# Attention's softmax weights divided before the product with v, whose result comes out as columns of x; even and odd heads in one step

## The chip, the core and the metric

The kernel runs on one core of one Trainium2 chip. Five engines work beside each other, each through its own instructions in order: PE (TensorE, the matrix array, with its weight loads shown apart as PEld), DVE (VectorE), ACT (ScalarE), POOL (GpSimd) and SP, which here only issues DMAs. The metric is the device time of one execution in microseconds (us); smaller is better. The kernel before takes 1169.96 us, the median of 3 runs (1168.95 to 1172.43).

## The reference

Three parts follow each other: attention, and two feed-forward parts, the second with a gate over 8 experts. Only attention is touched by the change. Its core, cut to what matters (B = 2, H = 8, S = 576, D = 64):

```python
def sm_attn(qq, kk, vv):                       # softmax over all keys
    s = scale * np.matmul(qq, kk.transpose(0, 1, 3, 2))
    a = np.exp(s - np.max(s, axis=-1, keepdims=True))
    a = a / (np.sum(a, axis=-1, keepdims=True) + 1e-09)
    return np.matmul(a, vv)
q_d = q.reshape(B, H, S // 4, 4, D).mean(axis=3)   # the same for k_d, v_d
out_up = np.repeat(sm_attn(q_d, k_d, v_d), 4, axis=2)       # "global": 144 averaged positions
mask = np.abs(pos[:, None] - pos[None, :]) < 4              # "local": 7 neighbours of each position
attn = ...                                                   # softmax of the masked scores, as above
return out_up + np.matmul(attn, v)
```

Its output, with heads and head dimension joined to 512 columns, is x (1152 rows). The first feed-forward part computes `h = x @ w_in`, `g = h * tanh(softplus(h))`, `g @ w_out`; its weights come as 64-bit floats. The second part takes most of the time and follows the first.

## The kernel before, in words

x is kept transposed, 512 columns as 4 groups of 128 partitions, split into a high and a low part (`xhi`, `xlo`). Its 1152 rows are 12 **tiles** of 96 rows; three tiles are a group of 288 columns, on which the first feed-forward part runs: `gemm1` (L531, 12 matmuls a step) and `gemm2` (L555, 12 matmuls a step), three steps later. Steps s = 0 to 17 work on the first three groups; group g can only start when attention has made its three tiles.

So attention is cut in four: three tiles are made in the **start**, before step 0. The other nine are made in three **waves** beside steps 0 to 5, 6 to 11 and 12 to 17. A list of steps (`attn_steps`, `hb_steps`, `piped`) is handed out between the matmuls of `gemm1` and `gemm2` by `pump`; a scheduler at build time then sets each engine's order. Between the attention steps of the start, 8 small matmuls of `identb` (L471) each keep PE at work. In the start the 64-bit weights are also rebuilt as 32-bit ones, by one ACT instruction (L185) and three on DVE (L186, L188, L190) for each half block, and split into two parts by ACT (L197) and POOL (L198); three buffers hold what DMA brings for it.

A **local unit** (`lunit`) is one tile and four heads of one parity, so two units make a tile. Even heads lie on partitions 0 to 63 of `qT` and `kT`, odd heads on 64 to 127. A unit has three steps: `sc` adds a mask and scores into one PSUM bank (L380, L383), takes row maxima on DVE (L307) and exponentials on ACT (L311, one per head); `tr` turns the weights on PE (L391) and copies them out on ACT (`pt`, L393); `av` multiplies with v (L398), and DVE takes the reciprocal of the sum and multiplies with it (L318, L319). The sum comes out of that product as a 65th column, since v has a column of ones (a row of 1e-9 is added for the reference's small term). The second unit of a tile has a fourth step, `fin`: four transposes (L409) bring x into columns, DVE adds the global part (L415), ACT and DVE make `xhi` and `xlo` (L416, L417).

A **global unit** (`gunit`) does the same for two heads of one parity and one half of a batch (L330, L342, L345, L354); four units make a half, and `gout` turns its result into columns (L364, `odT`).

Each fp32 matmul stands in the trace as two records, each transpose as one.

Of the kernel before, what the change touches and what calls it, by code (L numbers as in the profile page):

```python
# [24 lines left out]
PB = 3  # L25
# [11 lines left out]
def attn_moe_moe_kernel(  # L37
# [64 lines left out]

    vwt = [at.tile([W + 1, H, D + 1], F32, name=f"vw{i}", bufs=1) for i in range(VWB)]
    pl = [at.tile([TQ, H // 2, W + 1], F32, name=f"pl{i}", bufs=1) for i in range(PB)]
    pg = [at.tile([SH, 2, 2, SH + 1], F32, name=f"pg{i}", bufs=1) for i in range(PB)]
    for x in pl:
        POOL.memset(x[:, :, W:W + 1], 1.0)
    for x in pg:
        POOL.memset(x[:, :, :, SH:SH + 1], 1.0)
    for x in vwt:  # L110
        POOL.memset(x[96:W + 1, :, 0:D], 0.0)
        POOL.memset(x[96:W + 1, :, D:D + 1], 1e-9)
        POOL.memset(x[0:W, :, D:D + 1], 1.0)
# [112 lines left out]
    raw4, turned, kT, kd, qT, qd, vd, vw, od, odT, xt = ({} for _ in range(11))  # L226
# [30 lines left out]
    def load_vw(t):  # L257
        b, t6, lo, hi = window(t)
        vw[t] = vwt[t % VWB]
        for a, n in ((0, TQ), (TQ, W - TQ)):  # L260
            dma_kv(out=vw[t][a:a + n, :, 0:D], in_=v[b, :, lo + a:lo + a + n, :].rearrange("h p d -> p h d"))
# [26 lines left out]
    def prep_v(b, half):  # L288


        src = raw4["v", b, half]
        x = new(at, [SH + 1, H, D + 1], F32, "vd")
        POOL.memset(x[64:SH + 1, :, 0:D], 0.0)
        POOL.memset(x[64:SH + 1, :, D:D + 1], 2e-9)
        POOL.memset(x[0:SH, :, D:D + 1], 4.0)
        for i in range(2):
            a, z = x[:SH, 4 * i:4 * i + 4, 0:D], src[:, 4 * i:4 * i + 4]
# [3 lines left out]
        vd[b, half] = x  # L301

    def softmax_in(s3, p, n, scale, tag):

        nh = s3.shape[1]
        nm = new(at, [n, nh], F32, tag)
        DVE.tensor_reduce(out=nm, in_=s3, axis=AX.X, op=ALU.max, negate=True)  # L307
        if scale != 1.0:
            DVE.tensor_scalar(out=nm, in0=nm, scalar1=scale, scalar2=None, op0=ALU.mult)
        for i in range(nh):  # L310
            x = ACT.activation(out=p[i], in_=s3[:, i, :] if scale == 1.0 else s3[:, i, :].rearrange("p (c k) -> p c k", c=2),  # L311
                               func=AF.Exp, bias=nm[:, i:i + 1], scale=scale)
            exps.append(x)
# [7 lines left out]
    def gunit(b, half, heads):  # L321

        u = {}
        nh = len(heads)
        o = 64 * (heads[0] % 2)

        def sc():
            bk = at_bank()
            for i, h in enumerate(heads):
                PE.matmul(out=bk[:SH, SD * i:SD * i + SD], lhsT=qd[b, half][o:o + D, h // 2, :],  # L330
                          rhs=kd[b][o:o + D, h // 2, :], start=True, stop=True)
            s3 = bk[:SH, 0:nh * SD].rearrange("p (a b) -> p a b", b=SD)
            u["p"] = pg[state["pg"] % PB]
            state["pg"] += 1
            softmax_in(s3, [u["p"][:, i, :, 0:SH] for i in range(nh)], SH, 1.0 / 128.0, "gm")

        def tr():
            bk = at_bank()
            for i in range(nh):
                for c in range(2):  # L340
                    j = 2 * i + c
                    PE.transpose(out=bk[:SH + 1, SH * j:SH * j + SH], in_=u["p"][:, i, c, :],  # L342
                                 identity=ident[:SH, :SH])
            u["pt"] = new(at, [SH + 1, 2 * nh * SH], F32, "pt", 3)
            ACT.activation(out=u["pt"], in_=bk[:SH + 1, 0:2 * nh * SH], func=AF.Copy)  # L345

        def av():
            if (b, half) not in od:
                od[b, half] = new(at, [SH, H, D], F32, "od", 1)
            bk = at_bank()  # L350
            for i, h in enumerate(heads):
                for c in range(2):
                    j = 2 * i + c
                    PE.matmul(out=bk[:SH, (D + 1) * i:(D + 1) * (i + 1)], lhsT=u["pt"][:, SH * j:SH * j + SH],  # L354
                              rhs=vd[b, c][:, h, :], start=(c == 0), stop=(c == 1))
            o3 = bk[:SH, 0:nh * (D + 1)].rearrange("p (a b) -> p a b", b=D + 1)
            normalise(o3, SH, nh, od[b, half][:, heads[0]:heads[-1] + 1:2, :], "gd")
        return [sc, tr, av]

    def gout(b, half):  # L360
        bk = at_bank()
        src = od[b, half].rearrange("p h d -> p (h d)")
        for j in range(KD):
            PE.transpose(out=bk[:, SH * j:SH * j + SH], in_=src[:, 128 * j:128 * j + 128], identity=ident[:SH, :SH])  # L364
        t = new(at, [128, KD, SH], F32, "odT", 1)
        odT[b, half] = t
        ACT.activation(out=t.rearrange("p a b -> p (a b)"), in_=bk[:, 0:KD * SH], func=AF.Copy)

    def lunit(t, par):
# [4 lines left out]
        o = 64 * par  # L374
        u = {}

        def sc():
            bk = at_bank()
            s3 = bk[:TQ, 0:4 * W].rearrange("p (a b) -> p a b", b=W)
            PE.matmul(out=s3, lhsT=identb[:TQ, :TQ],  # L380
                      rhs=maskb[:TQ, m0:m0 + W].unsqueeze(1).to_broadcast([TQ, 4, W]), start=True, stop=False)
            for i in range(4):
                PE.matmul(out=s3[:, i, :], lhsT=qT[b, half][o:o + D, i, TQ * t3:TQ * t3 + TQ],  # L383
                          rhs=kT[b][o:o + D, i, lo:hi], start=False, stop=(i == 3))
            u["p"] = pl[(2 * t + par) % PB]
            softmax_in(s3, [u["p"][:, i, 0:W] for i in range(4)], TQ, 1.0, "lm")

        def tr():
            bk = at_bank()
            for i in range(4):  # L390
                PE.transpose(out=bk[:W + 1, TQ * i:TQ * i + TQ], in_=u["p"][:, i, :], identity=ident[:TQ, :TQ])  # L391
            u["pt"] = new(at, [W + 1, 4 * TQ], F32, "pt", 3)
            ACT.activation(out=u["pt"], in_=bk[:W + 1, 0:4 * TQ], func=AF.Copy)  # L393

        def av():
            bk = at_bank()
            for i in range(4):
                PE.matmul(out=bk[:TQ, (D + 1) * i:(D + 1) * (i + 1)], lhsT=u["pt"][:, TQ * i:TQ * i + TQ],  # L398
                          rhs=vw[t][:, 2 * i + par, :], start=True, stop=True)
            if t not in xt:  # L400
                xt[t] = new(at, [TQ, H, D], F32, "x", 3)
            normalise(bk[:TQ, 0:4 * (D + 1)].rearrange("p (a b) -> p a b", b=D + 1), TQ, 4,
                      xt[t][:, par:par + 7:2, :], "ld")

        def fin():
            bk = at_bank()
            src = xt[t].rearrange("p h d -> p (h d)")
            for j in range(KD):
                PE.transpose(out=bk[:, TQ * j:TQ * j + TQ], in_=src[:, 128 * j:128 * j + 128],  # L409
                             identity=ident[:TQ, :TQ])  # L410
# [7 lines left out]
        return [sc, tr, av] + ([fin] if par else [])  # L418

    def piped(units):  # L420

        n = max(len(u) for u in units)
        dl = 1 if state["start"] else 2
        return [units[i - dl * s][s] for i in range(len(units) + dl * n) for s in range(n)
                if 0 <= i - dl * s < len(units) and s < len(units[i - dl * s])]

    def hb_steps(hb):
# [14 lines left out]
        st += piped([gunit(b, half, hs) for hs in ([0, 2], [1, 3], [4, 6], [5, 7])])  # L442
        return st + [partial(gout, b, half)]

    def attn_steps(t0, t1):
        st, units = [], []
        for t in range(t0, t1):
            if t % 3 == 0:
                st += piped(units) if units else []
                st += hb_steps(t // 3)  # L450
                units = []
            if t >= VWB:
                st.append(partial(load_vw, t))
            units += [lunit(t, 0), lunit(t, 1)]
# [18 lines left out]
    def start_steps():  # L473
# [3 lines left out]
        near = {(t, par): lunit(t, par) for t in range(3) for par in range(2)}  # L477
        first = [near[t, par][:3] for t in range(2) for par in range(2)]
        far = [gunit(0, 0, hs) for hs in ([0, 2], [1, 3], [4, 6], [5, 7])]
        st = brought("k", 0, 0) + brought("q", 0, 0) + [first[0].pop(0), first[1].pop(0)] + brought("k", 0, 1)  # L480
        st += [partial(prep_v, 0, 0), partial(prep_v, 0, 1)]
        st += piped(first[:2] + [far[0], first[2], far[1], first[3], far[2], near[2, 0][:3], far[3], near[2, 1][:3]])
        return st + [partial(gout, 0, 0)] + [near[t, 1][3] for t in range(3)]
# [421 lines left out]
```

## Time and profile before

| | |
|---|---|
| median of 3 runs | 1169.96 us (1168.95 to 1172.43) |
| profiled execution | 1170.61 us, its span 1168.8 us |
| PE busy | 1116.5 us, 96% of the span |
| DVE, ACT, POOL busy | 639.9, 520.9, 420.9 us |
| start (0 to 74.1 us), waves (74.1 to 217.6 us) | first `gemm1` of steps 0 and 18 |
| mean granted TensorE clock | 0.977 of full speed |

The profile is one execution, taken by the hardware profiler. The time of this execution is its span plus what lies around it (1.8 us). Busy time of PE and PEld overlaps, and the durations of matmuls are longer than the distance from one to the next, since they are pipelined: what a row of matmuls costs is read from the starts of its neighbours.

### The profile page before, as it was taken

To read this page: it belongs to the slowest core of one execution; us is meant where nothing else is said; L and a number is where in the kernel's file an instruction comes from. 1 tells how busy PE (TensorE), PEld (TensorE's weight loads), DVE (VectorE), ACT (ScalarE), POOL (GpSimd) and SP (SyncE) were. 2 spreads that over 40 slices of the span, in tenths; PEclk is the share of its full clock that TensorE was granted. 3 is DMA by queue.
4 is the path that set the end of the run, shared out by engine and by line. 5 is a ranking of instruction groups with operands and counts; after the bars stand their busy time and mean duration, and the time that the engine had idled before them with its cause. 6 is when DMAs were issued, how large, how long until landed. Compare 5 with 4: busy or idle time off the path is not lost.

```text
span 1168.8 us, 19396 instructions
## 1 busy us (share of the span) xinstructions
PE 1116.5 (96%) x7418; PEld 1019.9 (87%) x7418; DVE 639.9 (55%) x1399; ACT 520.9 (45%) x1333; POOL 420.9 (36%) x479
## 2 busy tenths in 40 slices
PE   7979899879999799999999999999999999999998
PEld 6868788879999788898899988998899889988997
DVE  4884554696658976436444444364444544544342
ACT  3556556566566563342424424434244243342430
POOL 3622422462462642552514405225044052240500
PEclk9789999999999799999999999999999999999999
DMA  8474300041010210201102112011121120111102
GB/s 195 148 198 81 69 23 1 3 145 53 2 54 1 73 55 1 72 19 54 51 23 72 38 36 73 19 55 37 37 73 37 36 73 19 54 37 37 37 1 81
DMA packets 60201, 63.54 MB, mean 54 GB/s; under 512 B 24204, under 2 KB 44620, under 8 KB 60108
## 3 DMA queue, kind: packets, MB, share of 16 engines
q1 hardware_dynamic: 60108, 62.30, 18.4%
q8 instruction: 58, 0.95, 0.3%
q14 instruction: 35, 0.29, 0.1%
HBM read 59.93 MB, written 2.36 MB: 53 GB/s over the span
## 4 chain that ended last, share of the span: by engine, by line
PE 85%; DVE 7%; DMA 4%; issue 1%; ACT 1%; POOL 1%; SPq 0%; ACTq 0%; DVEq 0%; POOLq 0%
PE w L834 34%; PE acc L795 25%; PE w L531 8%; PE acc L555 7%; PE w L795 4%; PE w L383 1%; DMA vw<-in_v_dram 1%; DMA raw<-in_moe_w_out_dram 1%; DMA raw<-in_moe_w_in_dram 1%; PE w L398 1%; PE w L330 1%; DVE raw L190 1%; PE w L391 1%; DVE sums L689 1%; DVE raw L188 1%
## 5 line engine op out<-in xcount | busy, mean ns | idle before, releaser
L834 PE MATMUL w<-wc,hhi 128*128 128x512 f32 x1152 | 362.2, 392 | 0.0
L834 PEld LDWEIGHTS w<-wc,hhi 128*128 128x128 f32 x1152 | 213.6, 188 | 41.9
L834 PE MATMUL w<-wc,hlo 128*128 128x512 f32 x576 | 225.7, 392 | 0.0
L707 POOL TENSOR_TENSOR wc<-raw,wc 128x512 fp32r<-128x512 f32 x64 | 82.7, 1314 | 371.7 <-ACT wc L706 370.9
L795 PE MATMUL acc<-thi,wb 128*128 128x288 f32 x768 | 169.2, 295 | 1.1 <-ACT u L782 0.6
L795 PE MATMUL acc<-xhi,wb 128*128 128x288 f32 x768 | 166.6, 297 | 1.9 <-DVE hlo L787 1.3
L845 DVE SCALAR_TENSOR_TENSOR yacc<-w,P,yacc 128x512 f32<-128x512 f32 x126 | 94.3, 749 | 132.6 <-PE w L834 132.6
L795 PEld LDWEIGHTS acc<-xhi,wb 128*128 128x128 f32 x768 | 128.4, 189 | 3.9 <-DVE hlo L787 1.8
L795 PEld LDWEIGHTS acc<-thi,wb 128*128 128x128 f32 x768 | 128.5, 188 | 3.3 <-ACT u L782 0.8
L834 PEld LDWEIGHTS w<-wc,hlo 128*128 128x128 f32 x576 | 108.1, 188 | 24.1
L782 ACT ACTIVATE p<-acc 128x288 f32<-128x288 f32 x128 | 52.6, 412 | 164.8 <-PE acc L795 161.5
L786 ACT ACTIVATE hhi<-acc 128x288 fp32r<-128x288 f32 x128 | 52.8, 413 | 139.7 <-PE acc L795 117.6
L795 PE MATMUL acc<-xlo,wb 128*128 128x288 f32 x384 | 114.0, 297 | 0.0
L795 PE MATMUL acc<-tlo,wb 128*128 128x288 f32 x384 | 113.1, 295 | 0.0
L695 POOL TENSOR_TENSOR wb<-sums,wb 128x256 fp32r<-128x256 f32 x128 | 98.0, 786 | 15.6 <-ACT wb L694 8.6
L512 POOL TENSOR_SCALAR me<-me 128x288 f32<-128x288 f32 x64 | 62.5, 976 | 112.4 <-ACT me L511 100.7
L695 POOL TENSOR_TENSOR wb<-raw,wb 128x256 fp32r<-128x256 f32 x96 | 71.9, 752 | 75.3 <-PE acc L795 41.5
L787 DVE SCALAR_TENSOR_TENSOR hlo<-acc,hhi 128x288 fp32r<-128x288 f32 x128 | 58.0, 454 | 62.4 <-ACT hhi L786 62.0
L531 PE MATMUL w<-xhi,hi 128*128 128x288 f32 x256 | 78.9, 309 | 7.9 <-ACT xhi L416 4.7
L555 PE MATMUL acc<-glo,hi 128*128 128x288 f32 x256 | 76.5, 310 | 7.3 <-DVE glo L519 4.5
L531 PE MATMUL w<-xlo,hi 128*128 128x288 f32 x256 | 77.9, 305 | 0.1
L531 PE MATMUL w<-xhi,lo 128*128 128x288 f32 x256 | 77.5, 303 | 0.0
(196 smaller groups left out, 2174.6 us busy)
## 6 DMA issues: line engine op xcount, KB each, us to landing
raw<-in_moe_w_dram SPq DMA_DIRECT2D x64, 512.0 KB
raw<-in_moe_w_in_dram SPq DMA_DIRECT2D x16, 512.0 KB
raw<-in_moe_w_out_dram SPq DMA_DIRECT2D x16, 512.0 KB
vw<-in_v_dram SPq DMA_DIRECT2D x12, 192.0 KB
raw<-in_v_dram SPq DMA_DIRECT2D x8, 288.0 KB
raw<-in_q_dram SPq DMA_DIRECT2D x12, 144.0 KB
out_dram<-yacc SPq DMA_DIRECT2D x6, 256.0 KB
raw<-in_k_dram SPq DMA_DIRECT2D x2, 576.0 KB
```

Of the source, the lines that this page charges most:

```text
L188: DVE.scalar_tensor_tensor(out=x, in0=hi, scalar=0x80000000, in1=x, op0=ALU.bitwise_and, op1=ALU.bitwise_or)
L512: POOL.tensor_scalar(out=e, in0=e, scalar1=EXP20, scalar2=None, op0=ALU.min)
L531: PE.matmul(out=bk, lhsT=a[:, kk, o], rhs=b[:, kk, c0:c0 + n], start=(i == 0), stop=(i == 3 * KD - 1))
L555: PE.matmul(out=bk, lhsT=a[:, h, o], rhs=b, start=(first and i == 0), stop=(end and i == 2))
L695: POOL.tensor_tensor(out=t[:, 1], in0=src[u][w], in1=f32(t[:, 0]), op=ALU.subtract)
L707: POOL.tensor_tensor(out=t[:, 1], in0=r[:, a], in1=f32(t[:, 0]), op=ALU.subtract)
L782: ACT.activation(out=t, in_=bk[u, b], func=AF.Copy)
L786: ACT.activation(out=hi, in_=y, func=AF.Relu)
L787: DVE.scalar_tensor_tensor(out=lo, in0=y, scalar=0.0, in1=f32(hi), op0=ALU.max, op1=ALU.subtract)
L795: PE.matmul(out=bk[u, b], lhsT=wb[2 * h + u, w][:, wz, kk, :], rhs=ops[xz][:, k + kk, o + c:o + c + NP], start=(m in (0, 1, 5) and i == 0) ...
L834: PE.matmul(out=bk, lhsT=a[:, f, 128 * j:128 * j + 128], rhs=w[:, b, :], start=(i == 0), stop=(i == 3 * FH - 1))
L845: DVE.scalar_tensor_tensor(out=y, in0=bk, scalar=p, in1=y, op0=ALU.mult, op1=ALU.add)
```

## The change

The weights are divided by their sums before they are turned: ACT's exponentials give their sums as a second output (`accum_out`), DVE adds 1e-9 (and multiplies by 4 for the global part), takes the reciprocal and multiplies the weights in SBUF. So the columns of ones and the memsets for them go. The product with v then has v as the operand that is loaded (`lhsT`) and the turned weights as the one that streams; its result lies as columns, head dimension on partitions. Even heads are written to partitions 0 to 63 and odd heads to 64 to 127 of one PSUM bank, which is x's layout: `fin` and `gout` have nothing to turn and are part of `av` now. One unit has both parities; their matmuls alternate between the halves of the array, in the scores by rows and in the product with v by columns. So there are half as many units with twice as much in each, and a weights buffer more. `piped` puts a unit's steps two apart, latest step first, and the start has an order written out by hand. Fewer steps there bring fewer of the matmuls of `identb`.

The diff, cut to its core:

```diff
-PB = 3
+PB = 4
-    vwt = [at.tile([W + 1, H, D + 1], F32, name=f"vw{i}", bufs=1) for i in range(VWB)]
...
+    vwt = [at.tile([W, H, D], F32, name=f"vw{i}", bufs=1) for i in range(VWB)]
...
+    def softmax(s3, p, scale, rows, tag):
+        n, nh, nk = s3.shape
+        nm, den = new(at, [n, nh], F32, tag + "m", 4), new(at, [n, nh], F32, tag + "d", 4)
         DVE.tensor_reduce(out=nm, in_=s3, axis=AX.X, op=ALU.max, negate=True)
         if scale != 1.0:
             DVE.tensor_scalar(out=nm, in0=nm, scalar1=scale, scalar2=None, op0=ALU.mult)
         for i in range(nh):
+            exps.append(ACT.activation(out=p[:, i], in_=s3[:, i], func=AF.Exp, bias=nm[:, i:i + 1], scale=scale,
+                                       accum_out=den[:, i:i + 1]))
+        DVE.tensor_scalar(out=den, in0=den, scalar1=1e-9, scalar2=rows, op0=ALU.add, op1=ALU.mult)
+        DVE.reciprocal(out=den, in_=den)
+        DVE.tensor_tensor(out=p, in0=p, in1=den.unsqueeze(2).to_broadcast([n, nh, nk]), op=ALU.mult)
-    def normalise(o3, n, nh, dst, tag):
-        rec = new(at, [n, nh, 1], F32, tag)
-        DVE.reciprocal(out=rec, in_=o3[:, :, D:D + 1])
-        DVE.tensor_tensor(out=dst, in0=o3[:, :, 0:D], in1=rec.to_broadcast([n, nh, D]), op=ALU.mult)
...
+    def lunit(t):
         def sc():
+            s3 = [at_bank()[:TQ, 0:4 * W].rearrange("p (a b) -> p a b", b=W) for _ in range(2)]
+            for par in range(2):
+                PE.matmul(out=s3[par], lhsT=identb[:TQ, :TQ],
+                          rhs=maskb[:TQ, m0:m0 + W].unsqueeze(1).to_broadcast([TQ, 4, W]), start=True, stop=False)
+            for hp in range(HP):
+                for par in range(2):
+                    o = slice(64 * par, 64 * par + 64)
+                    PE.matmul(out=s3[par][:, hp, :], lhsT=qT[b, half][o, hp, TQ * t3:TQ * t3 + TQ],
+                              rhs=kT[b][o, hp, lo:hi], start=False, stop=(hp == HP - 1))
+            for par in range(2):
+                u[par] = pl[(2 * t + par) % PB]
+                softmax(s3[par], u[par], 1.0, 1.0, "l")
...
         def av():
             bk = at_bank()
+            for hp in range(HP):
+                for par in range(2):
+                    PE.matmul(out=bk[64 * par:64 * par + 64, TQ * hp:TQ * hp + TQ], lhsT=vw[t][:, 2 * hp + par, :],
+                              rhs=u["pt"][:, TQ * (4 * par + hp):TQ * (4 * par + hp) + TQ], start=True, stop=True)
...
     def piped(units):
-        n = max(len(u) for u in units)
-        dl = 1 if state["start"] else 2
-        return [units[i - dl * s][s] for i in range(len(units) + dl * n) for s in range(n)
-                if 0 <= i - dl * s < len(units) and s < len(units[i - dl * s])]
+        return [units[i - 2 * s][s] for i in range(len(units) + 4) for s in (2, 1, 0) if 0 <= i - 2 * s < len(units)]
```

Two places in the order of instructions matter below. The first is PE in the first wave, from the scores of its last tile on. Before: L380 and L383 are mask and scores, L391 turns weights (`pl`), L398 is the product with v (`vw`), L409 turns x.

```order
L380 MATMUL w<-maskb,identb 96x408
L383 MATMUL w<-kT,qT 96x102 x4
L391 MATMUL w<-ident,pl_94 103x96 x4
L398 MATMUL w<-vw_91,pt 96x65 x4
L391 MATMUL w<-ident,pl_95 103x96 x4
L398 MATMUL w<-vw_92,pt 96x65 x4
L391 MATMUL w<-ident,pl_96 103x96 x4
L398 MATMUL w<-vw_92,pt 96x65 x4
L409 MATMUL w<-ident,x 128x96 x4
```

After, at the same place (L356 and L361 mask and scores, L340 the global product with v, L372 turning weights, L379 the local product with v, L497 `gemm1`):

```order
L361 MATMUL w<-kT,qT 96x102 x4
L356 LDWEIGHTS identb
L356 MATMUL w<-maskb,identb 96x408
L361 MATMUL w<-kT,qT 96x102 x4
L340 MATMUL w<-pt,vd 64x72 x8
L372 MATMUL w<-ident,pl_94 102x96 x4
L372 MATMUL w<-ident,pl_95 102x96 x4
L379 MATMUL w<-pt,vw_91 64x96 x8
L372 MATMUL w<-ident,pl_96 102x96 x4
L372 MATMUL w<-ident,pl_97 102x96 x4
L497 MATMUL w<-xhi,hi_966 128x288
```

Between the last scores and the turning of that tile's weights (`pl_96`, `pl_97`) stand one global product, eight transposes and one local product with v; before, between a unit's scores and its own transposes (`pl_96`) stood eight transposes and two products of four matmuls.

The second is ACT at the end of the start: the instructions around the last `xhi` of the first group, for which step 0 waits. L185 (after: L176) is the first instruction of a rebuilt weight half, `raw_...` the buffer that a DMA fills for it. Before:

```order
L185 ACTIVATE raw<-raw_1098 128x512
L416 ACTIVATE xhi<-w 128x4x96
L416 ACTIVATE xhi<-acc 128x4x96
L185 ACTIVATE raw<-raw_1111 128x512
L416 ACTIVATE xhi<-w 128x4x96
L185 ACTIVATE raw<-raw_1117 128x512
```

After (L188 splits weights, L373 copies turned weights, L386 makes `xhi`):

```order
L176 ACTIVATE raw<-raw_885 128x512
L188 ACTIVATE hi_1043<-raw 128x512
L373 ACTIVATE pt<-w 102x384
L176 ACTIVATE raw<-raw_898 128x512
L386 ACTIVATE xhi<-acc 128x4x96
L176 ACTIVATE raw<-raw_904 128x512
```

Counted from the beginning of the program, 17 such weight halves stand ahead of the last `xhi` before, and 15 after.

## Rows read from the trace of the kernel before

**Rows 1.** The page's busy time of each engine (us, share of the span, instructions).

```profile
PE 1116.5 (96%) x7418; PEld 1019.9 (87%) x7418; DVE 639.9 (55%) x1399; ACT 520.9 (45%) x1333; POOL 420.9 (36%) x479
```

**Rows 2.** Busy time by stretch: start, its second part, waves; last columns clock, DMA.

```profile
26.60:74.10 47.50, 40.01 (x413) 35.00 (x413) 42.18 (x85) 28.09 (x68) 25.45 (x18) 0.79 0.54 161
74.10:217.60 143.50, 132.94 (x1118) 121.35 (x1118) 75.00 (x200) 81.65 (x238) 40.38 (x53) 0.95 0.26 56
217.60:269.00 51.40, 41.31 (x281) 38.88 (x282) 45.08 (x83) 33.34 (x76) 31.94 (x26) 0.97 0.34 108
```

**Rows 3.** Timeline of PE in the first wave: start us, duration us, instruction.

```profile
109.00 0.29 PE L531 MATMUL w<-xhi,lo 128*128 128x288 f32 x1
109.13 0.34 PE L380 MATMUL w<-maskb,identb 96*96 96x408 bf16 x1
109.40 0.94 PE L383 MATMUL w<-kT,qT 64*96 64x102 f32 x8
110.27 0.60 PE L391 MATMUL w<-ident,pl 96*103 96x96 f32 x4
...
112.88 0.55 PE L391 MATMUL w<-ident,pl 96*103 96x96 f32 x4
113.27 0.82 PE L398 MATMUL w<-vw,pt 103*96 103x65 f32 x8
113.92 0.50 PE L409 MATMUL w<-ident,x 96*128 96x96 f32 x4
```

**Rows 4.** Timeline of PE, global units of the first wave.

```profile
86.33 0.71 PE L330 MATMUL w<-kd,qd 64*72 64x144 f32 x4
86.97 0.48 PE L342 MATMUL w<-ident,pg 72*73 72x72 f32 x4
...
91.87 0.68 PE L354 MATMUL w<-vd,pt 73*72 73x65 f32 x8
92.39 0.43 PE L342 MATMUL w<-ident,pg 72*73 72x72 f32 x4
92.65 1.72 PE L354 MATMUL w<-vd,pt 73*72 73x65 f32 x24
```

**Rows 5.** Timeline of PE in the start: scores of both parities, even to acc, odd to w.

```profile
16.42 0.33 PE L383 MATMUL w<-kT,qT 64*96 64x102 f32 x1
16.43 0.33 PE L383 MATMUL acc<-kT,qT 64*96 64x102 f32 x1
16.59 0.25 PE L383 MATMUL w<-kT,qT 64*96 64x102 f32 x1
16.60 0.25 PE L383 MATMUL acc<-kT,qT 64*96 64x102 f32 x1
```

**Rows 6.** Groups on DVE in the waves: busy us, mean ns, then idle before.

```profile
L319 DVE TENSOR_TENSOR x<-w,ld 96x256 f32<-96x256 f32 x18 | 7.5, 419 | 0.5
L417 DVE TENSOR_TENSOR xlo<-w,xhi 128x384 fp32r<-128x384 f32 x9 | 4.9, 553 | 1.2 <-ACT xhi L416 1.1
L309 DVE TENSOR_SCALAR gm<-gm 72x2 f32<-72x2 f32 x12 | 3.6, 296 | 0.1
L318 DVE RECIPROCAL ld<-w 96x4 f32<-96x4 f32 x18 | 3.2, 178 | 11.8 <-PE w L398 11.6
```

**Rows 7.** Timeline of DVE and ACT behind the scores of 109.40.

```profile
110.44 0.58 DVE L307 TENSOR_REDUCE lm<-w 96x4 f32<-96x408 f32 x1 [3.19 <-PE w L383]
110.94 0.44 DVE L513 SCALAR_TENSOR_TENSOR mm<-me 128x288 f32<-128x288 f32 x1
...
111.35 1.03 ACT L311 ACTIVATE pl<-w,lm 96x102 f32<-96x102 f32 x4
```

**Rows 8.** Timeline of ACT at the end of the start.

```profile
70.32 0.67 ACT L185 ACTIVATE raw<-raw 128x512 f32<-128x512 f32 x1 [1.63 <-DMA raw<-in_moe_w_out_dram]
...
72.95 0.67 ACT L185 ACTIVATE raw<-raw 128x512 f32<-128x512 f32 x1 [1.21 <-DMA raw<-in_moe_w_in_dram]
73.53 0.47 ACT L416 ACTIVATE xhi<-w 128x384 fp32r<-128x384 f32 x1
```

More of the change, by code (lines that the diff above doesn't have):

```diff
@@ L101, in attn_moe_moe_kernel @@
                        compare_op=ALU.is_ge, fill=NEG)
[L103 to L113 removed]
+    vwt = [at.tile([W, H, D], F32, name=f"vw{i}", bufs=1) for i in range(VWB)]
+    pl = [at.tile([TQ, H // 2, W], F32, name=f"pl{i}", bufs=1) for i in range(PB)]
+    pg = [at.tile([SH, H // 4, SD], F32, name=f"pg{i}", bufs=1) for i in range(PB)]
     DVE.memset(two, 2.0)
@@ L327, in sc @@
         def sc():
-            bk = at_bank()
[L329 to L335, printed above, removed]
@@ L337, in tr @@
-        def tr():
-            bk = at_bank()
-            for i in range(nh):
-                for c in range(2):
[L341 to L357, printed above, removed]
@@ L358, in gunit @@
-        return [sc, tr, av]
[L360 to L369, printed above, removed]
+            bks = [at_bank() for _ in range(2)]
@@ new lines, in sc @@
+            for i, hp in enumerate(hps):
+                for par, bk in enumerate(bks):
+                    o = slice(64 * par, 64 * par + 64)
+                    PE.matmul(out=bk[:SH, SD * i:SD * i + SD], lhsT=qd[b, half][o, hp, :], rhs=kd[b][o, hp, :],
+                              start=True, stop=True)
+            for par, bk in enumerate(bks):
+                u[par] = pg[state["pg"] % PB]
+                state["pg"] += 1
+                softmax(bk[:SH, 0:2 * SD].rearrange("p (a b) -> p a b", b=SD), u[par], 1.0 / 128.0, 4.0, "g")
@@ new lines, in tr @@
+        def tr():
+            u["pt"] = new(at, [W, 8 * TQ], F32, "pt", 2)[:SH, 0:8 * SH].rearrange("p (a b) -> p a b", a=8)
+            for par in range(2):
+                bk = at_bank()
+                for i in range(2):
+                    for c in range(2):
+                        j = 2 * i + c
+                        PE.transpose(out=bk[:SH, SH * j:SH * j + SH], in_=u[par][:, i, SH * c:SH * c + SH],
+                                     identity=ident[:SH, :SH])
+                ACT.activation(out=u["pt"][:, 4 * par:4 * par + 4, :].rearrange("p a b -> p (a b)"),
+                               in_=bk[:SH, 0:4 * SH], func=AF.Copy)
@@ new lines, in av @@
+        def av():
+            if (b, half) not in odT:
+                odT[b, half] = new(at, [128, HP, SH], F32, "odT", 1)
+            bk = at_bank()
+            for i, hp in enumerate(hps):
+                for c in range(2):
+                    for par in range(2):
+                        PE.matmul(out=bk[64 * par:64 * par + 64, SH * i:SH * i + SH], lhsT=vd[b, c][:, 2 * hp + par, :],
+                                  rhs=u["pt"][:, 4 * par + 2 * i + c, :], start=(c == 0), stop=(c == 1))
+            ACT.activation(out=odT[b, half][:, hps[0]:hps[0] + 2, :].rearrange("p a b -> p (a b)"),
+                           in_=bk[:, 0:2 * SH], func=AF.Copy)
@@ L395, in av @@
         def av():
             bk = at_bank()
[L397 to L403, printed above, removed]
@@ L441, in hb_steps @@
                 st += [partial(load4, "k", b + 1, 0), partial(load4, "q", b + 1, 0), partial(load4, "k", b + 1, 1)]
-        st += piped([gunit(b, half, hs) for hs in ([0, 2], [1, 3], [4, 6], [5, 7])])
-        return st + [partial(gout, b, half)]
+        return st
     def attn_steps(t0, t1):
@@ L450, in attn_steps @@
                 st += hb_steps(t // 3)
-                units = []
+                units = [gunit(*divmod(t // 3, 2), i) for i in range(2)]
             if t >= VWB:
                 st.append(partial(load_vw, t))
-            units += [lunit(t, 0), lunit(t, 1)]
+            units.append(lunit(t))
         return st + piped(units)
```

67 lines of the change are left out of this document (22 added, 45 removed).

## Prediction

> **What bounds the kernel now.** I read the page's busy times first, then the stretches, then the timeline of PE. PE is busy for 96% of the span, DVE and ACT for about half [rows 1]: a saving on PE counts where PE sets the pace, and only there. The change touches two stretches [rows 2]. In the second part of the start (26.6 to 74.1 us) DVE is busy for 42.2 of 47.5 us and PE waits or runs filler matmuls: DVE and the weights that it rebuilds set the pace, and PE's savings are worth nothing. In the waves (74.1 to 217.6 us) PE is busy for 132.9 of 143.5 us, ACT for 81.7 and DVE for 75.0: here PE sets the pace, and a microsecond less of attention on PE is nearly a microsecond less of time, as long as the softmax keeps up. The stretch behind (217.6 to 269 us) is DVE's (45.1 of 51.4 us), with no attention in it. Its weights get their buffers only as the steps before it finish, so it should move forward with the end of the waves and not swallow the gain.
>
> **PE in the waves, a tile.** The cost of a batch is the distance from its start to the next one's. A local unit before takes 0.27 us for the mask (109.13 to 109.40), 0.87 for the scores (to 110.27), 0.39 for four transposes (112.88 to 113.27), 0.65 for the product with v (to 113.92) [rows 3]: 2.18 us. A tile has two, and the transposes of x: 0.50 long, less the 0.16 by which the four L391 outlast their step of 0.39, so 0.34. Together 4.70 us.
>
> After, a tile has two masks (0.54) and eight transposes (0.78) as before, and no transposes of x. Its scores alternate between the two row halves. The trace shows such a pair: two records start at 16.42 and 16.43, the next two at 16.59 and 16.60 [rows 5]. Both halves advance together, so I take 0.87 us for both parities instead of 1.74.
>
> The product with v alternates between column halves, which the trace nowhere shows. It is 16 records a tile. If two run together as in the scores, it takes the time of 8, 0.65 us; if they take turns, 1.30. To each I add 0.1 for the change of shape, about what the first distance in rows 5 (0.17) has over a later one (0.87 for eight, so 0.11). I take the lower bound, 0.75, since the nearest row is that of the row halves. A tile is then 2.94 us (upper bound 3.59), and saves 1.76 (1.11). Nine tiles in the waves: 15.8 us (10.0).
>
> The first distance bears on a rule of the Trainium skill, "TensorEngine Tiling (Array Packing)", Key Properties: a change of tiling mode drains TensorE. It speaks against the change, which adds 15 batches in column mode. With 0.3 us for each instead of 0.1 the saving would be 3 us smaller; no run here shows that drain by itself.
>
> **PE in the waves, a global half.** A unit before takes 0.64 us for scores (86.33 to 86.97), 0.26 for transposes (92.39 to 92.65), 0.52 for the product (91.87 to 92.39) [rows 4]. Four units and 0.26 for the four transposes of `gout`: 5.94 us. After there are two units: scores 0.64 (twice as many, in pairs), transposes 0.52, product 0.62 (upper bound 1.14), so 3.56 us in all (4.60). It saves 2.38 (1.34); three halves in the waves 7.1 us (4.0). PE's saving is 22.9 us, or 14.0 if column halves take turns.
>
> **What is late next: the softmax.** Before, the exponentials were all that stood between scores and transposes. Now a second parity, a sum, a reciprocal and a multiplication do too. Behind the scores that end at 110.27 the maximum starts at 110.44 and gives way at 110.94; four exponentials take 1.03 [rows 7]. With 0.1 between engines the even half's exponentials end 1.80 us after the scores. On DVE follow a small scalar instruction (0.30, as L309), a reciprocal (0.18, as L318) and the multiplication over 408 columns (about 0.58, estimated from the 0.553 of L417 over 384) [rows 6], 0.9 us as they overlap: 2.7 us. The odd half's exponentials end at 2.75, its weights are ready at 3.65.
>
> In the waves' last tile the order puts only the global product (0.62), eight transposes (0.78) and a local product (0.75) there: 2.15 us. The even transposes wait 0.55, the odd ones, due at 3.09, another 0.56: 1.1 us a wave with engines that are free. They are not: each step of the first feed-forward part puts instructions like L513 (0.44 [rows 7]) on the same queues. Two or three of these in the chain are 1.1 us. The wave's first tile and second global unit have about 4 and 3.5 us of cover, where I expect 0.5 each. That is 3.3 us a wave, 10 us in all; the bounds are 3.3 (free engines) and, below, 34. What is queued behind the waiting transposes is `gemm1` and all else on PE, so these waits count in full.
>
> Unknown is the sum that an exponential now gives. No second instruction for it stands in the order, so I take nothing; the upper bound is another distance of exponentials, 0.26 us each [rows 7].
>
> The multiplication read PSUM before and reads SBUF now. L309, on SBUF and four times smaller than anything else, takes 0.296 us on average against 0.178 of L318, which reads PSUM [rows 6]. The Trainium skill, "SBUF — State Buffer", Who interferes with whom, says that a DVE instruction with two SBUF inputs is blocked by a GpSimd instruction that reads SBUF, and that one SBUF input does not contend outside the two-port modes. By it the 30 multiplications of the waves would meet a POOL instruction in 28% of cases (40.4 of 143.5 us) for half of its 0.76 us (40.4 by 53) [rows 2], 3.2 us of DVE time; the sum would rise to 1160 at most if all of it were on the path.
>
> DVE's and ACT's totals stay below PE's: DVE gains 30 scalar instructions (9 us) and about 0.16 for each of 30 multiplications (5 us), 89 of some 130 us.
>
> **The start.** GEMM step 0 waits for the last `xhi`, 73.53, which stands on ACT behind a rebuilt weight half at 72.95 [rows 8]. These come every 2.63 us (70.32 to 72.95). After, two halves fewer stand ahead of it: up to 5.2 us earlier. Against it DVE, which is busy nearly all the time there, gets ten scalar instructions (3.0) and ten larger multiplications (1.6): up to 4.6 us later. I take 0. The memsets that go stand on POOL in the first microseconds, where DMA is what everything waits for; nothing.
>
> **Sum.** The profiled execution is 1170.6 us (span 1168.8 and 1.8 around it), 0.65 above the median. 1170.6 - 22.9 + 10 + 0 = 1157.7, and against the median 1157.
>
> **The rivals.**
> *Column halves take turns.* PE saves 14.0 instead of 22.9: 1170.0 - 14.0 + 10 = 1166 us. For it: no row shows column halves together. Against it: row halves do [rows 5].
> *The softmax is covered.* The waits stay at 1.1 us a wave, and with some of the two weight halves gained in the start the time is 1170.0 - 22.9 + 3.3 - 2 = 1148. For it: DVE and ACT are free for nearly half of the waves. Against it: they are in order.
> *Slower: each unit's transposes wait for the softmax.* The place is PE in front of the transposes of 15 units (five a wave). If an exponential with a sum takes 0.26 us more, a tile's chain gets 2.1 us longer and a global unit's 1.0. Then a wave waits 4.3 at the last tile, 2.6 at the first, 1.8 at the middle one (it has 5.0 of cover), 2.5 at the global units: 11.2, in three waves 34. 1170.0 - 22.9 + 34 = 1181. It decides from 1.5 us a unit on (22.9 by 15). For it: all of the new work lies between scores and transposes, in two queues that also carry the feed-forward part. Against it: no second instruction in the order.
> *The halves overlap nowhere in the waves*, so that the change doesn't do what it says: scores cost 0.70 more a tile and 0.64 a global unit, 10.1 in all, the product 8.9. 1170.0 - 3.9 + 10 = 1176. Against it stands rows 5 alone.
>
> **How the numbers follow.** Forecast 0.44, its own range 1151 to 1165; column halves in turns 0.18; covered 0.13; slower chain 0.17; no overlap 0.08. A measurement of this kernel tells about 0.3%, 3.5 us, from no change. Faster (below 1166.5): 0.42 + 0.10 + 0.13 = 0.65. Slower (above 1173.5): 0.14 from the chain, 0.05 from no overlap, 0.01 from turns, so 0.20. Within: 0.15. The range 1146 to 1174 takes in the covered case and column halves in turns, and leaves out most of the two slower ones.
>
> **What would show it.** In the profile after: pairs of L361 and of L379 that start within 0.02 us of each other (L379 decides the first rival); the waves shorter than 143.5 us by about 13, with PE's waits grown by about 10, put down to the multiplication of the weights (L301); an exponential still 0.26 us from the next (if 0.5, the slower rival); first `gemm1` within 5 us of 74.1. Wrong it would be if the waves keep their length, or if the stretch behind them grows by what they lose.

## The result, and the profile after

The changed kernel takes 1158.68 us (median of 4 runs, 1154.05 to 1160.08) against 1169.68 us of the kernel before beside it: the ratio is 0.9895, with an interval of 0.9861 to 0.9928. A second series of five (the run `again` below) gives 0.9899, 0.9884 to 0.9915. So it is 1% faster, 11 to 12 us, and the forecast of 1157 us is met. Two terms of its sum are not: each is wrong by about 10 us, with opposite signs.

First the stretches that answer to [rows 2], cut at the same places of the program (first `gemm1` of step 0 at 74.2 us, of step 18 at 206.0 us); the columns are start:end, length, busy us and instructions of PE, PEld, DVE, ACT and POOL, the granted clock, and DMA's share and GB/s:

```profile
26.60:74.20 47.60, 27.63 (x234) 22.78 (x234) 46.35 (x83) 28.15 (x89) 26.78 (x19) 0.57 0.46 145
74.20:206.00 131.80, 120.73 (x1070) 106.75 (x1071) 90.02 (x234) 88.46 (x338) 40.98 (x47) 0.95 0.30 67
206.00:257.00 51.00, 42.97 (x283) 40.81 (x281) 45.04 (x83) 33.64 (x78) 31.53 (x25) 0.90 0.35 107
```

The start is as long as before. The waves are 11.7 us shorter (13.5 in `again`, where they last 130.0), and the stretch behind them keeps its length. PE's busy time in the waves fell by 12.2 us (132.94 to 120.73; 118.61 in `again`), not by 22.9. Its time without work there (length less busy time) went from 10.6 to 11.1 us, not up by 10. The granted clock of the waves is 0.95 in both.

Wave by wave, from the same view:

```profile
74.20:122.30 48.10, 41.18 (x338) 36.68 (x339) 31.35 (x82) 28.89 (x109) 10.11 (x11) 0.86 0.59 127
122.30:167.30 45.00, 41.26 (x384) 36.22 (x382) 31.21 (x82) 31.92 (x120) 20.51 (x24) 1.00 0.23 55
167.30:206.00 38.70, 38.30 (x350) 33.85 (x351) 27.45 (x72) 27.65 (x110) 10.37 (x12) 1.00 0.03 7
```

The waves before, cut at the same steps (6 and 12):

```profile
74.10:121.40 47.30, 44.77 (x359) 40.14 (x360) 25.87 (x69) 25.95 (x75) 11.79 (x18) 0.92 0.55 116
121.40:172.70 51.30, 45.27 (x397) 41.53 (x395) 26.87 (x70) 29.09 (x86) 18.21 (x24) 0.97 0.21 48
172.70:217.60 44.90, 42.91 (x366) 39.68 (x366) 22.27 (x63) 26.61 (x78) 10.38 (x12) 0.96 0.01 1
```

The first wave gained nothing; the other two gained 6.3 and 6.2 us, and PE is at full clock in them. In the first, PE's busy time fell by 3.6 us (4.0 and 4.6 in the others), but its time without work grew from 2.5 to 6.9 us, and its clock is 0.86 instead of 0.92; the start ahead of it, with fewer filler matmuls, has 0.57 instead of 0.79.

What became of PE's part, at the end of the first wave. This answers to [rows 3]: start us, duration us, instruction, and the idle time before it with its releaser.

```profile
108.58 0.34 PE L356 MATMUL w<-maskb,identb 96*96 96x408 bf16 x1
108.85 0.94 PE L361 MATMUL w<-kT,qT 64*96 64x102 f32 x8
109.71 0.37 PE L356 MATMUL w<-maskb,identb 96*96 96x408 bf16 x1
110.02 0.94 PE L361 MATMUL w<-kT,qT 64*96 64x102 f32 x8
110.89 0.72 PE L340 MATMUL w<-pt,vd 72*64 72x72 f32 x16
111.95 0.87 PE L372 MATMUL w<-ident,pl 96*102 96x96 f32 x8 [0.35 <-ACT pl L297]
112.75 0.88 PE L379 MATMUL w<-pt,vw 102*64 102x96 f32 x16
113.85 0.54 PE L372 MATMUL w<-ident,pl 96*102 96x96 f32 x4 [0.22 <-ACT pl L297]
115.63 0.85 PE L372 MATMUL w<-ident,pl 96*102 96x96 f32 x4 [1.24 <-ACT pt L373]
```

Two things are to be seen. The product with v does overlap: 16 records take 0.88 us where eight took 0.82 [rows 3]. In the single records the two column halves start 0.006 us apart, then 0.076 to the next pair. The scores do not: the even heads' eight records, the second mask, then the odd heads' eight. Masks and scores take 2.31 us (108.58 to 110.89) instead of the 1.41 that I had counted. No local unit of the waves has a pair of scores that start together. Of the global ones only the first wave's two units have:

```profile
90.99 0.72 PE L314 MATMUL w<-kd,qd 64*72 64x144 f32 x8
...
136.47 0.71 PE L314 MATMUL w<-kd,qd 64*72 64x144 f32 x4
```

Eight records in 0.72 us there, four in 0.71 in the later waves (four such rows in each). Nine tiles by 0.90 and four global units by 0.64 are 10.7 us; 22.9 less 10.7 is 12.2, what PE's busy time fell by. That it agrees to a tenth is chance, since the same kernel's busy time is 2 us lower in `again`.

What became of the waits: the ones of PE in the waves that count (total us, times, longest):

```profile
PE w L262 <- DMA raw<-in_q_dram: 4.1, 1, 4.1
PE w L497 <- ACT xhi L386: 3.9, 2, 2.2
PE w L372 <- ACT pt L373: 1.2, 1, 1.2
...
PE w L372 <- ACT pl L297: 0.6, 2, 0.3
```

Only the 1.2 and 0.6 us in front of L372 belong to the softmax, all at the first wave's end. The wait for q was 0.4 us before. The loads of q for the first wave are issued from 76.19 us on, behind the last weight loads of the start; before it was from 71.92.

The chain itself is longer than I had it. The unit whose even scores end at 109.7:

```profile
109.82 0.58 DVE L293 TENSOR_REDUCE lm<-w 96x4 f32<-96x408 f32 x1 [0.80 <-PE w L361]
...
112.34 0.58 DVE L301 TENSOR_TENSOR pl<-pl,ld 96x408 f32<-96x408 f32 x1
...
114.91 0.57 DVE L301 TENSOR_TENSOR pl<-pl,ld 96x408 f32<-96x408 f32 x1
```

```profile
110.50 0.34 ACT L297 ACTIVATE pl<-w,lm 96x102 f32<-96x102 f32 x1 [1.25 <-DVE lm L293]
110.74 0.19 ACT L297 ACTIVATION_READ_ACCUMULATOR pl<-w,lm 96x1 f32 x1
110.83 0.33 ACT L297 ACTIVATE pl<-w,lm 96x102 f32<-96x102 f32 x1
...
111.70 0.20 ACT L297 ACTIVATION_READ_ACCUMULATOR pl<-w,lm 96x1 f32 x1
...
113.58 0.22 ACT L297 ACTIVATION_READ_ACCUMULATOR pl<-w,lm 96x1 f32 x1
...
115.11 0.52 ACT L373 ACTIVATE pt<-w 102x384 f32<-102x384 f32 x1
```

Even weights are ready at 112.92, 3.2 us behind their scores (forecast 2.7), odd ones at 115.48, 4.6 us behind theirs (forecast 3.65). Part of the reason is in the second block: an exponential with a sum is two instructions on ACT, 0.32 us from one exponential to the next instead of some 0.23 (four in 1.03 [rows 7]). But the weights are not what PE waits for longest. The last exponentials of a half unit end at 111.90 and 113.80, and with them a PSUM bank of scores comes free: the transposes that write it start at 111.95 and 113.85. Those at 115.63 start as the copy of earlier ones ends and frees theirs, 0.15 us behind the odd weights.

### The profile page after: what moved, and what is told of

It reads as the page before. It is cut to its first block, busy times and chain, and to the rows that moved or that the text cites. A ratio compares the mean times of both kernels' runs of the same rounds, so it can differ in the third digit from the quotient of the medians.

```text
span 1157.9 us, 19076 instructions
## 1 busy us (share of the span) xinstructions
PE 1094.9 (95%) x7202; PEld 995.9 (86%) x7202; DVE 663.2 (57%) x1439; ACT 528.7 (46%) x1465; POOL 419.0 (36%) x452
## 4 chain that ended last, share of the span: by engine, by line
PE 81%; DVE 9%; DMA 3%; issue 2%; ACT 2%; POOL 1%; SPq 0%; DVEq 0%; POOLq 0%; ACTq 0%
PE w L800 34%; PE acc L761 26%; PE w L497 7%; PE acc L521 6%; PE w L761 4%; PE w L361 1%; DVE raw L179 1%; DMA vw<-in_v_dram 1%; DVE raw L181 1%; DMA raw<-in_moe_w_out_dram 1%; DMA raw<-in_moe_w_in_dram 1%; DVE sums L655 1%; DVE mm L479 1%; DVE raw L177 1%; DVE t L561 1%
## 5 line engine op out<-in xcount | busy, mean ns | idle before, releaser
L811 DVE SCALAR_TENSOR_TENSOR yacc<-w,P,yacc 128x512 f32<-128x512 f32 x126 | 94.3, 749 | 131.8 <-PE w L800 131.8
L497 PE MATMUL w<-xhi,hi 128*128 128x288 f32 x256 | 79.4, 311 | 3.9 <-ACT xhi L386 3.9
L779 DVE TENSOR_TENSOR w<-w,p 128x288 f32<-128x288 f32 x64 | 29.5, 462 | 88.6 <-PE w L761 45.6
L497 PE MATMUL w<-xlo,hi 128*128 128x288 f32 x256 | 78.2, 306 | 0.5 <-DVE xlo L387 0.4
```

Of the source, the lines that this page charges most:

```text
L497: PE.matmul(out=bk, lhsT=a[:, kk, o], rhs=b[:, kk, c0:c0 + n], start=(i == 0), stop=(i == 3 * KD - 1))
L779: DVE.tensor_tensor(out=bk[u, "D"], in0=bk[u, "D"], in1=kept[u, "p1"], op=ALU.add)
L811: DVE.scalar_tensor_tensor(out=y, in0=bk, scalar=p, in1=y, op0=ALU.mult, op1=ALU.add)
```

## The experiments

All are edits of the changed kernel, timed in five rounds beside the kernel before. Ratios are to that kernel; 0.001 is 1.2 us. The build sets each engine's order anew for each kernel; what that shifted is said where it matters.

**again.** The changed kernel, unedited.

> The changed kernel once more, word for word, as the measure for the runs beside it: 1157 to 1160 us.

1158.23 us, 0.9899 (0.9884 to 0.9915). The others are read against this.

**pair.** The scores of the waves are chained so that they alternate as the code has them:

```diff
+            prev = mk                       # the second mask
             for hp in range(HP):
                 for par in range(2):
-                    PE.matmul(out=s3[par][:, hp, :], ...)
+                    with (ExitStack() if state["start"] else tc.issue_after(prev.ins)):
+                        prev = PE.matmul(out=s3[par][:, hp, :], ...)
```

(The global scores in the same way.)

> The scores of the waves are made to stand even, odd, even, odd on PE (in the changed kernel the order puts all four even heads of a local unit, then the second mask, then all four odd heads). Theory A, PE's count decides: nine local units save 0.87 us each and four global units 0.64 us each, 10.4 us, so about 1148 us. Theory B, the softmax behind the scores decides: the even half's chain starts later and the cover shrinks by as much as PE saves, so more than half is given back, 1154 us or more.

1162.64 us, 0.9934 (0.9921 to 0.9946): 4 us slower, not 10 faster. Theory A falls; B holds and was still too mild. The waves, and the waits of PE that grew:

```profile
74.20:208.40 134.20, 116.05 (x1070) 101.43 (x1071) 88.02 (x234) 88.52 (x339) 40.96 (x47) 0.92 0.30 66
```

```profile
PE w L376 <- ACT pl L297: 3.2, 4, 1.3
PE acc L525 <- POOL glo L489: 2.7, 3, 1.3
PE acc L525 <- ACT ghi L488: 2.3, 5, 0.8
...
PE w L358 <- ACT pl L297: 0.8, 1, 0.8
PE w L501 <- ACT pl L297: 0.7, 1, 0.7
```

PE is busy for 4.7 us less, and without work for 18.2 us instead of 11.1. The clock is 0.92 instead of 0.95. It is a mean of full and half speed, so it stands for 21 us at half speed instead of 13 (16% of 134.2 us, 10% of 131.8), and some 4 us of the PE time saved went there. One place, in the third wave; PE, then ACT, then DVE:

```profile
189.59 0.94 PE L365 MATMUL w<-kT,qT 64*96 64x102 f32 x16
190.47 0.72 PE L342 MATMUL w<-pt,vd 72*64 72x72 f32 x16
191.12 0.54 PE L376 MATMUL w<-ident,pl 96*102 96x96 f32 x4
192.96 0.54 PE L376 MATMUL w<-ident,pl 96*102 96x96 f32 x4 [1.30 <-ACT pl L297]
193.34 0.34 PE L358 MATMUL w<-maskb,identb 96*96 96x408 bf16 x1
194.43 0.33 PE L358 MATMUL w<-maskb,identb 96*96 96x408 bf16 x1 [0.76 <-ACT pl L297]
```

```profile
192.71 0.20 ACT L297 ACTIVATION_READ_ACCUMULATOR pl<-w,lm 96x1 f32 x1
...
194.16 0.22 ACT L297 ACTIVATION_READ_ACCUMULATOR pl<-w,lm 96x1 f32 x1
```

```profile
188.57 0.58 DVE L301 TENSOR_TENSOR pl<-pl,ld 96x408 f32<-96x408 f32 x1
...
190.90 1.06 DVE L293 TENSOR_REDUCE lm<-w 96x4 f32<-96x408 f32 x2
```

Both parities' scores are done at 190.47, in half the time. Both then hold a PSUM bank until ACT has read them, one after the other: the even half to 192.91, the odd one to 194.38. The transposes at 192.96 start when the first bank comes free (the weights that they turn, of an earlier unit, were ready at 189.15), the second mask at 194.43 when the other does. So the waits are there, and on these rows it is the front of the softmax that makes them, with the banks that it holds, and not the division at its end.

**pairbare.** Theory after pair: the softmax's added work eats what PE saves. So pair again, with the softmax cut short in the waves (no sums, no scalar instruction, no reciprocal, no multiplication; the weights stay undivided there):

```diff
             exps.append(ACT.activation(out=p[:, i], ..., scale=scale,
-                                       accum_out=den[:, i:i + 1]))
+                                       **({"accum_out": den[:, i:i + 1]} if state["start"] else {})))
+        if state["start"]:
             DVE.tensor_scalar(out=den, ...); DVE.reciprocal(out=den, in_=den)
             DVE.tensor_tensor(out=p, in0=p, in1=den..., op=ALU.mult)
```

> Scores alternate in all units of the waves as in the run pair; in the waves the exponentials give no sums, and the sums' scalar instruction, the reciprocal and the multiplication of the weights are left out (the start keeps them), so a half unit's chain behind the scores is as short as in the kernel before, 1.3 us shorter than in pair. Theory A, pair lost its gain to waits for the softmax: most of the 7 us by which PE's idle time in the waves grew goes, and some of the clock with it, 1148 to 1155 us. Theory B, what holds pair up is not the chain but PSUM banks and the instructions queued on ACT: 1159 us or more.

1152.9 us, 0.9869 (0.9847 to 0.9892): 9.7 us below pair, the intervals apart.

```profile
73.80:196.60 122.80, 110.85 (x1070) 98.64 (x1070) 61.68 (x144) 80.03 (x243) 40.17 (x47) 0.93 0.33 72
```

Theory A. PE's time without work in the waves is 12.0 us, and its busy time 9.9 us below that of the profile after (7.8 below `again`), near the 10.4 us at which the alternating scores were priced. The time is only some 4 to 5 us below that of the changed kernel (0.9869 against 0.9899), and no run has the short softmax without alternating scores, so what it gives by itself is not known. Leaving the work out shortens the chain, empties the queues (DVE's busy time falls by 26 us against pair, ACT's by 8) and frees the banks earlier, all at once: which of these counts most the run does not tell, and by the rows of pair B's banks have a part in it.

**nonormw.** The multiplication alone is left out in the waves, with the scores as in the changed kernel (`if state["start"]:` ahead of L301; the order on PE stays nearly the same).

> Leaves out the multiplication of the weights by the reciprocal of their sums in the waves only (the start keeps it), so the weights are ready 0.5 to 1.4 us earlier. Theory A, the softmax is covered but for the first wave, where PE waited 2.2 us for it: at most 2 us faster, 1156 to 1159. Theory B, as predicted, the longer chain costs about 10 us in the waves: 1149 to 1152.

1158.31 us, 0.9895 (0.9878 to 0.9912): nothing. Theory A. With scores that don't alternate, the multiplication costs no time that can be measured; it stands behind the exponentials, which free the banks.

**dbl.** The multiplication twice in the waves (a second L301).

> In the waves the weights are multiplied by the reciprocal of their sums twice instead of once, which changes the result but makes the chain behind the scores 0.5 to 0.7 us longer for each of 30 half units. Theory A, there is slack behind the scores in most units, as the run without the multiplication showed at the other end: at most 3 us slower, 1158 to 1161. Theory B, the chain stands at the edge of its cover, and each further 0.5 us is paid at half of the units or more: 1166 us or more.

1171.51 us (1164.05 to 1182.63), 1.0019 (0.9994 to 1.0044): 13 us slower at the median, with a wide spread. By its time, theory B: taking one multiplication away is worth nothing, and a version with one more takes 0.4 us longer for each of the 30 half units. But the build changed PE's order in many places here: one local unit of the first wave and two global units of the later ones now alternate, and in `pairg` a change of order of that kind costs 4 us by itself. So that the changed kernel stands at the edge of its cover fits this run, and is not shown by it.

**pair3.** More cover for pair: a unit's steps three units apart, `PB = 6`, `units[i - 3 * s][s]`.

> Scores made to alternate as in the run pair, and a unit's three steps stand three units apart instead of two, with six weights buffers instead of four. Theory A, what pair saved on PE (some 10 us) went into waits for the softmax, for want of cover: with more cover PE's waits in the waves fall from 18 us to about 12 and the time to 1150 to 1156. Theory B, PE's waits in pair come from ACT and DVE being late altogether, or the longer tail of three steps costs what the cover gains: 1160 to 1165, as pair.

1172.99 us, 1.0025 (1.0012 to 1.0039). Both theories are too low.

The waves last 144.1 us. PE is without work for 23.7 us of them, and its clock is 0.88. The waits are spread over `ghi`, `glo` and `pl`; which comes first stays open. Cover was not bought by distance alone; that the longer tail brings its own waits is likely, and not shown.

**pairg.** Only the global scores alternate.

> Only the scores of the global units are made to alternate between row halves in all waves; the local ones keep the order of the changed kernel. Theory A, PE's count decides: four units save 0.64 us each, 2.6 us, about 1155.6 us. Theory B, holding back the even half until the odd bank is free makes PE wait as long: 1158 us or more.

1162.55 us, 0.9938 (0.9922 to 0.9955). By its time, theory B; but the build moved local units as well (one of them now alternates), so it does not price the global scores by themselves.

**turns.** The product with v, all even heads ahead of the odd ones:

```diff
-            for hp in range(HP):
-                for par in range(2):
+            for par in range(2):
+                for hp in range(HP):
                     PE.matmul(out=bk[64 * par:64 * par + 64, ...
```

> The product with v keeps its two column halves, but all matmuls of even heads stand before those of odd heads, so the halves can't run beside each other. Theory A, the overlap of column halves is a main part of the gain: a local product costs 0.65 us more and a global one 0.45, in the waves 9 by 0.65 and 6 by 0.45, 8.5 us, so about 1167 us. Theory B, the product stands where PE would wait anyway: under 3 us more, 1159 to 1161.

1164.51 us, 0.9947 (0.9931 to 0.9964): 5 to 6 us slower. Theory A, at two thirds of its price:

```profile
109.22 1.02 PE L340 MATMUL w<-pt,vd 72*64 72x72 f32 x16
111.08 1.26 PE L379 MATMUL w<-pt,vw 102*64 102x96 f32 x16
```

A local product takes 0.38 us more, a global one 0.30; by 9 and by 6 that is 5.2 us. It is less than twice the time, since the odd half starts (111.47) while the even half's last four records still go (the last at 111.71).

**nonorms.** The multiplication left out in the start only.

> Leaves out the multiplication of the weights by the reciprocal of their sums in the start only. It is 6.0 us of VectorE's 46.4 busy us there. Theory A, VectorE sets the pace of the start and its extra work ate what the two weight halves fewer ahead of the last xhi gave: the first gemm1 comes 3 to 6 us earlier and the time falls to 1153 to 1156. Theory B, the start waits for transfers (the weight loads), and VectorE's gaps only move: within 2 us.

1158.31 us, 0.9906 (0.9886 to 0.9925): no gain. But the first `gemm1` comes at 67.2 us, against 74.2 in the profile after and 73.0 in `again`:

```profile
26.60:67.20 40.60, 27.31 (x229) 21.03 (x229) 38.22 (x69) 26.65 (x88) 23.60 (x18) 0.62 0.45 145
67.20:120.00 52.80, 40.64 (x339) 35.72 (x339) 36.48 (x89) 30.49 (x112) 11.59 (x12) 0.81 0.58 136
```

```profile
PE w L262 <- DMA raw<-in_q_dram: 9.2, 1, 9.2
```

Theory A is right on the start (VectorE sets its pace; 6 to 7 us came free), and wrong on the time: PE then waits 9.2 us for q, and the first wave ends at 120.0, between the 119.4 of `again` and the 122.3 of the profile after.

**qfirst.** The other way round: q and k ahead of the last two weight loads (`last["w0"]` set one weight load earlier).

> The loads of q and k for the first wave no longer queue behind the last two weight loads of the start. Theory A, the first wave gained nothing because PE waits 4.1 us for q behind those loads and its clock then falls: the first wave gets 3 to 5 us shorter, 1154 to 1156 us. Theory B, the DMA wait only takes the place of a wait for the rebuilt weights (gemm step 1 or 2 waits as long): within 1.5 us of 1158.7.

1160.76 us, 0.9917 (0.9901 to 0.9933): no gain, and half a us above what theory B allowed.

```profile
72.20:118.90 46.70, 42.70 (x338) 37.56 (x339) 32.25 (x83) 28.45 (x109) 9.93 (x11) 0.86 0.63 129
```

The third step of `gemm1` (s = 2) comes at 81.9 us instead of 87.5 in `again`, but the wave is as long as there (46.4 us): PE has 3.2 us less without work, and as much more busy time at a clock of 0.86. The single rows show what took the wait's place. In `again` the matmuls of `gemm1` stand 0.24 us apart (half clock; 0.13 is full) on both sides of the wait, from 74.4 to 84.4 us. Here they reach 0.13 at 78.4, but behind a gap from 79.1 to 81.9, in which PE has only small transposes and waits for DVE, they are back at 0.24 until 84.9. So the wait for q alone was not what the first wave lost.

**poolqf.** Both together: the early q, and the start's multiplication on POOL.

> In the start the multiplication of the weights by the reciprocal of their sums runs on POOL instead of VectorE, and the loads of q and k for the first wave stand ahead of the last two weight loads. Theory A, the two runs that freed one of both gained nothing because the other held: leaving out the multiplication brought the first gemm1 6 us forward but PE then waited 9.2 us for q, and the earlier q found the start unchanged. With both, the second step of gemm1 comes some 5 us earlier and stays so: 1153 to 1155 us. Theory B, what is gained at the beginning of the first wave is lost by its end (TensorE's lower clock, PSUM banks, values of v that arrive no earlier): 1157 to 1160 us.

1162.26 us (1156.64 to 1166.12), 0.9938 (0.9919 to 0.9956). Neither theory; a transpose of the start now waits 5.1 us for POOL, and the first `gemm1` comes at 77.9 us.

**warm16.** `WARM1 = 16`.

> Twice as many matmuls of identb between the steps of the start (16 instead of 8), so that TensorE idles less there; in the changed kernel its granted clock is 0.57 of full speed from 26.6 to 74.2 us and 0.86 in the first wave. Theory A, the first wave pays for the clock it inherits: with more filler it gets 2 to 4 us shorter, 1155 to 1157. Theory B, the clock in the first wave falls because of the wait for q at 78 us, whatever came before: no change, within 1.5 us.

1162.39 us (1159.12 to 1174.85), 0.995 (0.9924 to 0.9975): slower, which neither theory said. In the profiled execution, the longest, the first `gemm1` comes at 80.8 us. That the filler itself holds up the start is likely, and not shown.

None of the versions that compute everything beats the changed kernel.

## Why the prediction was right, and where it was not

*What bounds the kernel* held: only the waves changed length by more than 1.1 us, and nothing was swallowed behind them (51.0 us against 51.4).

*PE in the waves, a tile and a global half* is the step that failed. "Both halves advance together, so I take 0.87 us for both parities instead of 1.74" holds in the start [rows 5], for two of its three tiles after the change, and in two of the waves' six global units. In the other four, and in all nine tiles, the build puts the even heads' matmuls, the odd bank's mask, the odd heads' matmuls. The order of the changed kernel that stands ahead of the prediction says so (L361 x4, L356, L361 x4), and I priced the code instead of that order. It cost 10.7 of the 22.9 us. The rival "halves overlap nowhere" was true of most scores (it priced them at 0.70 us more a tile, where the prediction's own rows give 0.87 and the profile after 0.90), and untrue of the product with v, whose term (0.75 and 0.62 us) was right; `turns` shows that its overlap is worth 5 to 6 us of the 11.

*What is late next* was mis-sized for this kernel, 10 us for 2, and about right in size for the one that I had priced. I let both chains begin behind the last scores. As the scores stand, the even chain begins 1.2 us earlier, and PE spends 0.9 us a tile more in front of the transposes. With alternating scores (`pair`) the waits come: PE's time without work grows by 7.1 us, and the lower clock takes about 4 more. So the two errors are tied: time that PE spends on separate scores is cover for the softmax. `pairbare` shows the other side, since with a short softmax alternating scores come out 9.7 us faster than in `pair`. That the errors have opposite signs is no accident; that they cancel to 1 or 2 us, so that 1157 is met, is luck. The place was wrong, too: I expected waits put down to the multiplication (L301). In `pair` none is; 5 of the 7 us are put down to exponentials (L297), which hold the banks, and most of the rest to the `ghi` and `glo` of the feed-forward part.

*Accumulate of exp 0* was too low: it is 0.09 us each (0.32 for 0.23), within the bounds of 0 and 0.26.

*The start 0* was right (74.2 against 74.1 us; 73.0 in `again`). Of the balance that it was argued from, DVE's side is shown: without the multiplications the first `gemm1` comes 6 to 7 us earlier, and DVE's busy time there grew by 4.2 us (42.18 to 46.35) where up to 4.6 was counted. What the two weight halves fewer give, no run shows by itself. What the step left out is what follows: loads of weights that wait for DVE's rebuilding held the loads of q back by 4.3 us, PE waited for them, and its clock was lower than before. With the wait gone (`qfirst`) the first wave is no shorter, so why it gained nothing stays open; the lower clock, in the start and behind the waits, is the rival, and `warm16` did not settle it.

*DVE against POOL*: in the waves a multiplication over 408 columns takes 0.691 us on average, 0.58 where it runs undisturbed, in the start 1.103:

```profile
L301 DVE TENSOR_TENSOR pl<-pl,ld 96x408 f32<-96x408 f32 x18 | 12.4, 691 | 0.5
```

```profile
153.68 0.80 DVE L301 TENSOR_TENSOR pl<-pl,ld 96x408 f32<-96x408 f32 x1
```

```profile
153.62 0.92 POOL L478 TENSOR_SCALAR me<-me 128x288 f32<-128x288 f32 x1 [4.47 <-ACT me L477]
```

That is some 2 us of DVE time over 18 of them (0.11 each), off the path, as `nonormw` shows. The rows point to POOL: the 13 that no POOL instruction overlaps take 0.57 to 0.58 us, and the five that one overlaps take 0.80 to 1.22, which is the whole 2 us. Of the 12 global multiplications six are overlapped, and two of these take no longer than the others; no run took POOL's instructions away. (The prediction called L309 four times smaller than anything else; by [rows 6] it has 2 columns against the 4 of L318, so it is half as wide.)

*The slower rival* (transposes that wait at each unit) did not happen here; with one more multiplication of 0.6 us a half unit (`dbl`) the gain is gone, though not by the chain alone, since PE's order changed as well.

## What to carry to other kernels

Price the order that the build writes, not the loop in the code: matmuls that are written alternately overlap fully only if they stand alternately on the engine. PE time saved between a producer and its consumer on other engines is also cover lost, so a saving should be entered together with the wait that it uncovers; that a chain costs nothing when it is shortened does not say that it may grow for nothing. Count the PSUM banks that are held until another engine has read them, not only the values that are waited for. When a stage gets shorter, look at what is queued behind its last transfer before counting the gain.

## What the runs showed of the hardware

- Two products that write different column halves run beside each other (starts 0.006 us apart), and where the code puts four matmuls of one half ahead of four of the other (`turns`), the second half begins 0.24 us before the first half's last record starts.
- An exponential that also gives a sum leaves a second record on ACT; the distance grows from 0.23 to 0.32 us.
- PE's clock couples waits and work: in the waves of pair and pair3, 7 and 13 us more without work went with a granted clock of 0.92 and 0.88 instead of 0.95, so there the waits cost more than their length. It is not the sum of the waits alone: in `pairbare` 12.0 us without work went with 0.93.
- A DVE multiplication of 408 columns in SBUF takes 0.57 to 0.58 us with POOL idle, and 0.80 to 1.22 in the five cases of the waves that a POOL instruction overlaps.
